# Linear attention and a two-layer network on one core: two of seven products one pair ahead, attention's product for two heads at once, new half steps

## The chip, the core and the metric

The kernel runs on one core of a Trainium2 chip. The metric is device time in microseconds (us). Five engines run beside each other, each through its own instructions in their written order: TensorE (PE in the profile; PEld is its weight load), VectorE (DVE), ScalarE (ACT), GpSimd (POOL) and SyncE (SP), which issues nearly all transfers (DMA).

## The reference

```python
q_s = exp(q - max(q, -1)); q_s = q_s / (sum(q_s, -1) + 1e-09)      # softmax over 64 features
k_s = exp(k - max(k, 2));  k_s = k_s / (sum(k_s, 2) + 1e-09)       # softmax over 576 tokens
kv  = einsum('bhsd,bhse->bhde', k_s, v)
x   = einsum('bhsd,bhde->bhse', q_s, kv)    # 8 batches, 8 heads, 576 x 64, as (4608, 512)
out = relu(x @ w_in) ** 2 @ w_out           # w_in 512 x 2048, w_out 2048 x 512
```

All data are float32.

## The kernel before, in words

A number is held as a high and a low part (both `float32r`), and a product is three matmuls: high by high, high by low, low by high. Tokens go in blocks of 512: block b is the first 512 tokens of batch b for b = 0 to 7, and block 8 holds the 64 that are left of each batch. The 16 chunks `fc` of 128 hidden features go through `x @ w_in`, relu, square and `@ w_out`.

Stages. The first phase (a list written by hand) loads and splits the weights and does attention for batches 0 and 1 and all of block 0. Block 1 takes one chunk a step: twelve matmuls of 512 columns for `h` (`h_part`), relu (ACT, L518), square (DVE, L519), split into `g_hi` (ACT, L524) and `g_lo` (DVE, L529), and two steps later twelve matmuls into the four output accumulators (`o_part`). Blocks 2 to 8 take two chunks, a *pair*, in one iteration, eight iterations a block. There `x @ w_in` goes by a scheme with seven products instead of eight, over sums and differences of weights (`s2`, `s34`, and a part of `wi` that is overwritten, built by `sum_units` on POOL, DVE and ACT during block 1) and of tokens (`combo_units`). Each product, B11, T1, B21, T2, T3, B22 and T4, is six matmuls of 256 columns (`times`, L866). They gather in three banks of PSUM: `A` (bank0), `Bk` (bank1), `E` (bank2). An iteration of before runs B11 into `A`, T1 into `E`; then ACT copies `A` into `Bk` (L917, the *seed*) and `E` into `e5` (L918); then B21 goes on in `A` and T2 in `Bk`, `u2` is copied from `Bk` (L924), T3 goes on in `Bk` and B22 in `E`; DVE adds `Bk`+`e5` and `E`+`u2` into the upper halves (L931, L932); relu and Square on ACT (L934, L938) finish chunk a. T4 goes on in `Bk`, and `relu_square` (L518, L519) finishes chunk b. Between these stand eight `triple`s, each three matmuls of 512 columns (L541 to L543), of the pair before.

Attention for batches 2 to 7 runs one block ahead, in *units* (`k_max`, `q_exp`, `parts`, ...) put at *slots* (half steps): four slots an iteration, `in_slot(slot)` to `in_slot(slot + 3)`. Two heads are a pair of 128 partitions, and two such pairs a *couple*, whose `kv` product stands at slots 2 and 16 of a block (`COUPLES`); all other slots are counted from there (`UNIT_AT`, `NINTH_AT`). The maximum of `k` over tokens needs twelve small DVE instructions per pair (`k_bound`, `k_spread`). `q` goes through a 32 x 32 transpose, out to memory and back (`q_turn`, `q_out`, `q_back`). `q_split` then splits each head's 64 partitions and puts high and low parts on opposite halves of the 128, `parts` stacks the factors likewise, and one matmul per head gives the main product in the lower and the correction in the upper 64 partitions. `joined` copies the correction (ACT, L465) and adds it (DVE, L467).

Weights of the second layer are kept in memory as split parts and streamed back through a ring of three buffers, thirteen of sixteen chunks a block (`STREAMED`, `load_out`); `s34` comes back through two buffers, one iteration after the last use of its buffer (`load_s34`).

Of the kernel before, what the change touches and what calls it, by code (L numbers as in the profile page):

```python
# [42 lines left out]
S34_AT = "o1", "o3"  # L43
SUMS_AT = 5, 9, 12, 15, 19, 22, 25, 29
# [65 lines left out]
def attention_ffn_kernel(ctx: ExitStack, tc: tile.TileContext, q, k, v, w_in, w_out, out):  # L110
# [88 lines left out]
    nc.gpsimd.memset(kvs[HALF:, 0, D:].bitcast(F32), 0.0)  # L199
    nc.gpsimd.memset(kvs[:HALF, 1, D:].bitcast(F32), 0.0)  # L200
# [43 lines left out]
    stage = {}  # L244
# [63 lines left out]
    def sum_units(p):  # L308
# [24 lines left out]
        def high_parts():  # L333
# [3 lines left out]
            s34[p] = place(S34_AT[p % 2], [P, 2, 512], "s34")  # L337
# [27 lines left out]
    def attention(b, pr):  # L365
# [7 lines left out]
        def k_max():  # L373
            st["m"] = attn_pool.tile([P, 2, D], F32, name="m")
            nc.vector.tensor_reduce(st["m"], kk.rearrange("p h j d -> p h d j"), axis=AX.X, op=ALU.max)

# [605 lines left out]
```

## Time and profile before

| | |
|---|---|
| median of 3 runs | 999.57 us (998.36 to 1000.91) |
| the profiled execution | 997.45 us |
| its span, first to last instruction | 995.4 us |
| PE busy | 878.0 us (88%), 5367 matmuls |
| DVE, ACT, POOL busy | 625.7 (63%), 507.2 (51%), 276.7 us (28%) |
| granted TensorE clock, mean | 0.964 of 2.4 GHz |
| moved by DMA | 164.06 MB, mean 165 GB/s |

Busy time of an engine is the time in which at least one of its instructions ran. Matmuls are pipelined, so the distance between two starts is shorter than the time of one, and a PE that is busy throughout can still be working below its best rate. The waits name what ended an engine's idle time.

### The profile page before, as it was taken

The page shows a single profiled execution, that of the slowest core. Times are in us where ns is not written, and L with a number is a line of the kernel's source. Part 1 is how long each engine was busy: PE and PEld are TensorE (multiplying, and loading weights), DVE is VectorE, ACT ScalarE, POOL GpSimd, SP SyncE. Part 2 cuts the span into 40 slices and gives each one's busy share as a digit, 9 for nine tenths or more (in the row PEclk, how much of TensorE's full clock was granted, in tenths as well). Part 3 has the DMA queues.
Part 4 walks back from the last instruction along what each step waited for, and adds up shares of the span by engine and source line. Part 5 has one row for each costly group of instructions (what it writes and reads, how often), then busy time and mean ns, then how long its engine had stood idle before and what let it go on. Part 6 is the DMA issues. An engine that isn't in the chain of part 4 may idle for free.

```text
span 995.4 us, 15293 instructions
## 1 busy us (share of the span) xinstructions
PE 878.0 (88%) x5367; PEld 748.0 (75%) x5367; DVE 625.7 (63%) x1273; ACT 507.2 (51%) x1038; POOL 276.7 (28%) x233
## 2 busy tenths in 40 slices
PE   8999998687768989888878989788878999999997
PEld 7777886475667877777667877777767888998996
DVE  8888879779756576657766576557776433333222
ACT  5988535354435554445544654545444544434333
POOL 5777615465411221111221221111221220111000
PEclk9999999798879999899979999999989999999999
DMA  9999345455545555555555555554544446445431
GB/s 257 282 308 238 106 143 164 141 181 176 160 132 181 156 178 158 172 158 152 163 143 192 160 179 141 174 173 149 169 136 158 131 128 186 153 132 165 148 123 47
DMA packets 124555, 164.06 MB, mean 165 GB/s; under 512 B 51776, under 2 KB 92736, under 8 KB 124480
## 3 DMA queue, kind: packets, MB, share of 16 engines
q1 hardware_dynamic: 123808, 162.41, 54.7%
q8 instruction: 42, 0.69, 0.3%
q10 hardware_dynamic: 672, 0.69, 0.2%
q14 instruction: 33, 0.27, 0.1%
HBM read 132.38 MB, written 30.67 MB: 164 GB/s over the span
## 4 chain that ended last, share of the span: by engine, by line
PE 54%; DVE 20%; ACT 13%; issue 5%; DMA 3%; POOL 2%; SPq 2%; ACTq 0%; POOLq 0%; DVEq 0%
PE bank L866 20%; PE o_ps L541 9%; PE o_ps L542 9%; PE o_ps L543 9%; ACT g_hi L524 3%; DVE r L519 2%; DVE staged L467 2%; DVE g_lo L529 2%; DVE qn L413 2%; ACT corr L465 2%; DMA qT<-bounce 1%; ACT qs L455 1%; PE bank L513 1%; PE bank L514 1%; PE bank L512 1%
## 5 line engine op out<-in xcount | busy, mean ns | idle before, releaser
L543 PE MATMUL o_ps<-wo,g_lo 128*128 128x512 f32 x576 | 231.8, 402 | 11.5 <-DVE g_lo L529 11.5
L541 PE MATMUL o_ps<-wo,g_hi 128*128 128x512 f32 x576 | 235.1, 408 | 4.9 <-ACT g_hi L524 4.9
L542 PE MATMUL o_ps<-wo,g_hi 128*128 128x512 f32 x576 | 233.1, 405 | 0.0
L529 DVE TENSOR_TENSOR g_lo<-r,g_hi 128x512 fp32r<-128x512 f32 x128 | 99.7, 779 | 103.3 <-ACT g_hi L524 102.6
L866 PE MATMUL bank<-B,wi 128*128 128x256 f32 x672 | 104.3, 292 | 51.2 <-ACT bank L917 51.2
L866 PEld LDWEIGHTS bank<-B,wi 128*128 128x128 f32 x672 | 93.3, 193 | 68.6 <-ACT bank L917 63.1
L543 PEld LDWEIGHTS o_ps<-wo,g_lo 128*128 128x128 f32 x576 | 112.5, 195 | 42.5 <-DVE g_lo L529 16.9
L541 PEld LDWEIGHTS o_ps<-wo,g_hi 128*128 128x128 f32 x576 | 114.2, 198 | 22.2 <-ACT g_hi L524 6.0
L456 POOL TENSOR_TENSOR qs<-qT,qs 64x640 fp32r<-64x640 f32 x48 | 77.5, 1615 | 189.9 <-ACT qs L455 168.9
L542 PEld LDWEIGHTS o_ps<-wo,g_hi 128*128 128x128 f32 x576 | 113.1, 196 | 15.0
L866 PE MATMUL bank<-T,wi 128*128 128x256 f32 x672 | 101.1, 286 | 17.3 <-DVE bank L931 17.3
L934 ACT ACTIVATE r<-bank 128x512 f32<-128x512 f32 x56 | 33.6, 599 | 162.0 <-DVE bank L932 162.0
L866 PE MATMUL bank<-T,s 128*128 128x256 f32 x672 | 104.3, 294 | 12.2 <-DMA s<-s_kept 8.6
L866 PEld LDWEIGHTS bank<-T,wi 128*128 128x128 f32 x672 | 89.6, 190 | 27.3 <-DVE bank L931 24.3
L866 PEld LDWEIGHTS bank<-T,s 128*128 128x128 f32 x672 | 95.2, 200 | 17.2 <-issue 8.9
L524 ACT CAST g_hi<-r 128x512 fp32r<-128x512 f32 x128 | 79.5, 621 | 46.3 <-DVE r L519 39.4
L467 DVE TENSOR_TENSOR staged<-bank,corr 64x320 f32<-64x320 f32 (+1 forms) x96 | 43.0, 448 | 88.4 <-ACT corr L465 88.1
L931 DVE TENSOR_TENSOR bank<-bank,uu 128x256 f32<-128x256 f32 x56 | 23.8, 424 | 103.4 <-PE bank L866 103.2
L263 POOL TENSOR_TENSOR B<-staged,B 128x512 fp32r<-128x512 f32 x21 | 27.8, 1323 | 204.6 <-ACT B L259 126.8
L465 ACT COPY corr<-bank 64x320 f32<-64x320 f32 (+1 forms) x96 | 38.1, 396 | 71.8 <-PE bank L461 48.0
L924 ACT COPY uu<-bank 128x256 f32<-128x256 f32 x56 | 20.8, 371 | 64.0 <-PE bank L866 64.0
L519 DVE TENSOR_TENSOR r<-r,bank 128x512 f32<-128x512 f32 x72 | 48.9, 680 | 6.1 <-ACT r L518 6.0
(186 smaller groups left out, 1464.1 us busy)
## 6 DMA issues: line engine op xcount, KB each, us to landing
wo<-out_kept SPq DMA_DIRECT2D x91, 512.0 KB, 3.6
s<-s_kept SPq DMA_DIRECT2D x56, 512.0 KB, 4.2
bounce<-tb SPq DMA_DIRECT2D x28, 320.0 KB, 2.4
qT<-bounce SPq DMA_DIRECT2D x104, 80.0 KB, 3.8
raw_i<-in_moe_w_in_dram SPq DMA_DIRECT2D x16, 512.0 KB, 6.7
raw_o<-in_moe_w_out_dram SPq DMA_DIRECT2D x16, 512.0 KB, 8.4
out_dram<-o SPq DMA_DIRECT2D x64, 128.0 KB, 2.5
out_kept<-wo SPq DMA_DIRECT2D x13, 512.0 KB, 3.7
```

The lines of the kernel that those rows point to most:

```text
L263: nc.gpsimd.tensor_tensor(t[:, 1], src, t[:, 0].bitcast(F32), op=ALU.subtract)
L456: nc.gpsimd.tensor_tensor(qs[other], src, qs[own].bitcast(F32), op=ALU.subtract)
L465: nc.scalar.copy(corr[half[h]], ps[HALF:])
L467: nc.vector.tensor_tensor(dst, ps[:HALF], corr[half[h]], op=ALU.add)
L519: nc.vector.tensor_tensor(r, r, ps, op=ALU.mult)
L524: nc.scalar.copy(g_hi, r)
L529: nc.vector.tensor_tensor(g_lo, r, g_hi.bitcast(F32), op=ALU.subtract)
L541: nc.tensor.matmul(acc, g_hi[:, ts], wo[fc][:, 0], start=(n == 0), stop=False)
L542: nc.tensor.matmul(acc, g_hi[:, ts], wo[fc][:, 1], start=False, stop=False)
L543: return nc.tensor.matmul(acc, g_lo[:, ts], wo[fc][:, 0], start=False, stop=(n == NFC - 1))
L866: nc.tensor.matmul(dst, lhs, rhs, start=start and c == n == 0, stop=c == 1 and n == 2, skip_group_check=True)
L934: nc.scalar.activation(ra, A, AF.Relu)
```

## The change

1. B11 and T1 of the next pair run inside this iteration (`ahead`): B11 after the fifth triple, T1 behind T4. `seed` follows chunk b's relu on ACT. An iteration starts with T2, B21, B22; T3 stands between the second and third triple. Chunk b's square goes from DVE to ACT (Square), in blocks 2 to 8 always and in block 1 for every second chunk. `e5` and `u2` have fixed buffers (`spare`).
2. Attention's product takes two heads at once: `kvs` holds two block-diagonal 128 x 128 factors (high and low), `q_high` and `q_low` split all 128 partitions in one instruction each, three matmuls gather in PSUM (L453), and one ACT copy per product (L454) takes the place of `joined`.
3. `k_bound` and `k_spread` run once per couple, over 256 columns, and DVE's four small copies are reductions now (`k_stats`).
4. All units and loads have new slots (`FORMER`, `LATTER` and three tables for the first couples). The sums of weights of pairs 5 to 7 move from block 1 to block 2.
5. `s34` has three buffers and is loaded an iteration earlier; chunk 6 of the second layer is streamed too (fourteen of sixteen).

The core of the diff (line numbers of the change in the text are those of the changed kernel):

```diff
-COUPLE_AT = {1: (6, 18)}
-COUPLES = 2, 16
-STREAMED = tuple(fc for fc in range(16) if fc not in (6, 14, 15))
+COUPLES = {1: (6, 17)}, (2, 15)
+STREAMED = tuple(fc for fc in range(16) if fc not in (14, 15))
-S34_AT = "o1", "o3"
-SUMS_AT = 5, 9, 12, 15, 19, 22, 25, 29
+S34_AT = "o1", "o3", "o6"
+S34_BUILT = 0, 1, 0, 1, 2, 2, 0, 1
+SUMS_AT = tuple((s, s + 2, s + 3, s + 4) for s in (5, 9, 13, 17, 21, 39, 43, 47))
...
-    parts=(0, 5), low0=(3, 8), low1=(4, 9), high=(5, 11), k_less=(-7, -1), k_exp=(-6, -1), q_split=(1, 5), k_max=(-13, -8),
...
+    k_max=(-17, -14), q_max=(-16, -9), q_less=(-16, -8), q_exp=(-15, -7), q_sum=(-13, -5), q_norm=(-10, -4),
...
     def load_s34(i):
-        if i < NFC // 2 * (B - 1):
+        if i not in (5, 6, 7) and i < NFC // 2 * (B - 1):
             p = i % (NFC // 2)
-            t = s34[p] = place(S34_AT[i % 2], [P, 2, 512], "s34")
+            t = s34[p] = place(S34_AT[i % 3], [P, 2, 512], "s34")
...
-        def product(h, ps, g0, nj):
-            qs = st["q"][h][:, :nj, g0 : g0 + 2].rearrange("p j g a -> p j (g a)")
-            nc.tensor.matmul(ps.rearrange("p (j i) -> p j i", j=nj), kvs[:, h], qs, start=True, stop=True)
-
-        def joined(h, ps, corr, at):
-            n = ps.shape[1]
-            nc.scalar.copy(corr[half[h]], ps[HALF:])
-            dst = staged(b, pr // 2)[half[h], at : at + n]
-            nc.vector.tensor_tensor(dst, ps[:HALF], corr[half[h]], op=ALU.add)
+        def product(g0, nj, at):
+            n = nj * HALF
+            ps = bank(n)
+            for i, (k, x) in enumerate(((0, 0), (0, 1), (1, 0))):
+                rhs = st["q"][x][:, :nj, g0 : g0 + 2].rearrange("p j g a -> p j (g a)")
+                dst = ps.rearrange("p (j i) -> p j i", j=nj)
+                nc.tensor.matmul(dst, kvs[:, k], rhs, start=(i == 0), stop=(i == 2))
+            nc.scalar.copy(staged(b, pr // 2)[:, at : at + n], ps)
...
-    def relu_square(ps):
+    def relu_square(ps, by_act):
         r = work.tile([P, NT], F32, name="r")
         nc.scalar.activation(r, ps, AF.Relu)
-        nc.vector.tensor_tensor(r, r, ps, op=ALU.mult)
+        if by_act:
+            nc.scalar.activation(r, r, AF.Square)
+        else:
+            nc.vector.tensor_tensor(r, r, ps, op=ALU.mult)
         return r
...
+                following = (blk, p + 1) if p + 1 < NFC // 2 else (blk + 1, 0)
+                times(Bk[:, low0], lambda i: s2[p][:, i], blk, "T2", False)
+                times(A[:, low0], lambda i: wi[fa][:, i, QUAD:], blk, "B21", False)
+                times(E[:, low0], lambda i: s34[p][:, i, QUAD:], blk, "B22", False)
+                nc.scalar.copy(u2, Bk[:, low0])
                 triple(0)
                 in_slot(slot)
+                tt(A[:, low1], E[:, low0], u2, op=ALU.add)
+                triple(1)
                 times(Bk[:, low0], lambda i: s34[p][:, i, :QUAD], blk, "T3", False)
                 tt(Bk[:, low1], Bk[:, low0], e5, op=ALU.add)
                 ra = work.tile([P, NT], F32, name="r")
                 nc.scalar.activation(ra, A, AF.Relu)
+                triple(2)
+                in_slot(slot + 1)
+                triple(3)
                 triple(4)
+                ahead(*following, 1)
                 nc.scalar.activation(ra, ra, AF.Square)
                 ga = low_part(*high_part(ra))
+                in_slot(slot + 2)
                 times(Bk[:, low0], lambda i: wi[fb][:, i, QUAD:], blk, "T4", False)
-                rb = relu_square(Bk)
+                ahead(*following, 5)
+                rb = work.tile([P, NT], F32, name="r")
+                nc.scalar.activation(rb, Bk, AF.Relu)
+                seed(following[0])
+                triple(5)
+                in_slot(slot + 3)
+                nc.scalar.activation(rb, rb, AF.Square)
                 triple(6)
                 triple(7)
+                load_s34((blk - 2) * (NFC // 2) + p + 3)
```

What moves on PE, at the passage from one iteration to the next in a middle block. Before, B11 and T1 (into bank0 and bank2) open the iteration, one triple follows, then B21 and T2:

```order
L541 MATMUL o_ps3_5020<-wo3_5052,g_hi_5153 128x512
L542 MATMUL o_ps3_5020<-wo3_5052,g_hi_5153 128x512
L543 MATMUL o_ps3_5020<-wo3_5052,g_lo_5170 128x512
L461 MATMUL bank3_90<-qs1_5146,kvs_96 128x320
L866 MATMUL bank0_87<-B11_4164,wi6_705 128x256 x6
L866 MATMUL bank2_89<-T1_4250,wi7_807 128x256 x6
L541 MATMUL o_ps0_5017<-wo4_5129,g_hi_5238 128x512
L542 MATMUL o_ps0_5017<-wo4_5129,g_hi_5238 128x512
L543 MATMUL o_ps0_5017<-wo4_5129,g_lo_5240 128x512
L866 MATMUL bank0_87<-B21_4654,wi6_705 128x256 x6
L866 MATMUL bank1_88<-T2_4718,s2_1963 128x256 x6
```
With the change, B11 of the next pair stands behind the fifth triple and T1 behind T4; `q_hi` and `q_lo` in the last rows are attention's product in three passes:

```order
L552 MATMUL o_ps0_4745<-wo3_4790,g_hi_4849 128x512
L553 MATMUL o_ps0_4745<-wo3_4790,g_hi_4849 128x512
L554 MATMUL o_ps0_4745<-wo3_4790,g_lo_4851 128x512
L877 MATMUL bank0_87<-B11_3974,wi6_705 128x256 x6
L877 MATMUL bank1_88<-T4_4564,wi5_628 128x256 x6
L877 MATMUL bank2_89<-T1_4080,wi7_807 128x256 x6
L552 MATMUL o_ps1_4746<-wo3_4790,g_hi_4849 128x512
L553 MATMUL o_ps1_4746<-wo3_4790,g_hi_4849 128x512
L554 MATMUL o_ps1_4746<-wo3_4790,g_lo_4851 128x512
L453 MATMUL bank3_90<-q_hi_4899,kvs_96 128x320
L453 MATMUL bank3_90<-q_lo_4900,kvs_96 128x320
L453 MATMUL bank3_90<-q_hi_4899,kvs_96 128x320
```
Between T1 and the next matmul that needs a seed (T2 now, B21 before) stood one triple; now three triples and, here, attention's product stand there.

On ACT, before, from the relu of chunk b (bank1) to the seeds, at the start of iteration 2 of a block (`corr` is the correction of attention's product, `kvs` its factors, `qs0` and `qs1` the split `q`):

```order
L518 ACTIVATE r_5120<-bank1_88 128x512
L465 COPY corr_5054<-bank3_90 64x256 x2
L240 CAST kvs_96<-kf_4943 64x64
L447 CAST kvs_96<-kf_4943 64x64
L240 CAST kvs_96<-kf_4943 64x64
L447 CAST kvs_96<-kf_4943 64x64
L455 CAST qs0_5143<-qT_97 64x640
L455 CAST qs1_5146<-qT_97 64x640
L524 CAST g_hi_5153<-r_5120 128x512
L917 COPY bank1_88<-bank0_87 128x256
L918 COPY uu_5155<-bank2_89 128x256
```
And with the change, from the relu of chunk a (bank0) to the copy of `u2`:

```order
L958 ACTIVATE r_4769<-bank0_87 128x512
L454 COPY staged0_4777<-bank3_90 128x320
L407 ACTIVATE qn_4756<-qn_4756 128x640
L964 ACTIVATE r_4769<-r_4769 128x512
L535 CAST g_hi_4802<-r_4769 128x512
L454 COPY staged0_4777<-bank3_90 128x256
L970 ACTIVATE r_4830<-bank1_88 128x512
L933 COPY bank1_88<-bank0_87 128x256
L934 COPY spare0_1528<-bank2_89 128x256
L974 ACTIVATE r_4830<-r_4830 128x512
L535 CAST g_hi_4849<-r_4830 128x512
L950 COPY spare0_1528<-bank1_88 128x256
```
The two seeds (bank1 from bank0, `spare0` from bank2) stood behind eight instructions of attention and the split of chunk b; they now come straight behind chunk b's relu, and the split of chunk b comes after them.

On DVE, before, the seven instructions of attention and of the token sums between `g_lo` of one iteration and the two additions (L931, L932) of the next:

```order
L529 TENSOR_TENSOR g_lo_4708<-r_4668,g_hi_4691 128x512
L426 TENSOR_TENSOR qn_4526<-qn_4526,qs_4624 128x640
L281 TENSOR_TENSOR staged0_3927<-staged1_4424,staged0_3927 128x512
L283 TENSOR_TENSOR staged0_3927<-staged0_3927 128x256 x2
L430 STREAM_TRANSPOSE tb_4745<-qn_4526 128x5x4x32
L413 TENSOR_TENSOR qn_4749<-qt1_84,qm_4689 128x2x5x64
L287 TENSOR_TENSOR staged1_4424<-staged1_4424,staged0_3927 128x512
L931 TENSOR_TENSOR bank1_88<-bank1_88,uu_4693 128x256
L932 TENSOR_TENSOR bank0_87<-bank2_89,uu_4693 128x256
```
With the change, from one pair of additions (L953, L956) to the next:

```order
L953 TENSOR_TENSOR bank0_87<-bank2_89,spare0_1528 128x256
L956 TENSOR_TENSOR bank1_88<-bank1_88,spare0_1528 128x256
L421 STREAM_TRANSPOSE tb_4389<-qn_4174 128x5x4x32
L399 TENSOR_REDUCE qm_4393<-qt1_84 128x10
L540 TENSOR_TENSOR g_lo_4415<-r_4383,g_hi_4413 128x512
L392 TENSOR_TENSOR kt1_80<-kt1_80,spare1_1529 128x640
L404 TENSOR_TENSOR qn_4424<-qt1_84,qm_4393 128x2x5x64
L287 TENSOR_TENSOR staged0_3735<-staged1_4167,staged0_3735 128x512
L289 TENSOR_TENSOR staged0_3735<-staged0_3735 128x256 x2
L540 TENSOR_TENSOR g_lo_4464<-r_4438,g_hi_4462 128x512
L953 TENSOR_TENSOR bank0_87<-bank2_89,spare0_1528 128x256
L956 TENSOR_TENSOR bank1_88<-bank1_88,spare0_1528 128x256
```
The additions now stand right behind `g_lo` here, and the units that stood ahead of them lie after the additions of the iteration before.

## Rows read from the trace of the kernel before

**Rows 1.** Windows: first phase, block 1, blocks 2, 4, 6 and 8.
```profile
core 0: us, PE busy (x) PEld busy (x) DVE busy (x) ACT busy (x) POOL busy (x), PEclk, DMA share, GB/s
0.00:126.46 126.46, 123.16 (x712) 98.84 (x712) 105.74 (x196) 97.19 (x182) 87.53 (x86) 1.00 0.84 234
126.46:238.66 112.20, 95.54 (x457) 76.81 (x456) 92.23 (x177) 50.35 (x104) 56.22 (x47) 0.92 0.48 157
238.66:367.78 129.12, 99.11 (x625) 84.79 (x624) 86.35 (x175) 59.50 (x127) 30.89 (x25) 0.92 0.57 167
480.54:593.68 113.14, 96.53 (x625) 82.76 (x624) 74.60 (x164) 57.35 (x122) 22.71 (x18) 0.95 0.55 164
706.37:814.55 108.18, 95.81 (x625) 82.64 (x624) 63.21 (x141) 56.66 (x122) 23.33 (x18) 0.97 0.47 143
899.01:983.40 84.39, 84.39 (x530) 76.23 (x529) 24.63 (x44) 33.18 (x68) 1.29 (x1) 1.00 0.39 120
```

**Rows 2.** Windows, same columns: iteration 0 of block 2, iteration 2 of block 4.
```profile
238.66:261.07 22.41, 15.03 (x108) 12.70 (x106) 20.42 (x41) 8.91 (x21) 10.84 (x10) 0.77 0.63 202
508.94:526.72 17.78, 12.90 (x71) 11.37 (x70) 10.69 (x21) 8.31 (x19) 3.08 (x2) 0.81 0.53 163
```

**Rows 3.** Timeline of PE: where two iterations of block 7 start (start us, us).
```profile
867.36 0.88 PE L866 MATMUL bank<-B,wi 128*128 128x256 f32 x6
877.90 0.88 PE L866 MATMUL bank<-B,wi 128*128 128x256 f32 x6
```

**Rows 4.** Timeline of PE: attention's products in block 4, and what follows them.
```profile
490.47 0.80 PE L500 MATMUL bank<-vt,ke 128*64 128x65 f32 x20
...
491.78 0.98 PE L866 MATMUL bank<-T,wi 128*128 128x256 f32 x6
...
506.42 0.31 PE L461 MATMUL bank<-qs,kvs 128*128 128x320 f32 x1
506.57 0.92 PE L866 MATMUL bank<-T,wi 128*128 128x256 f32 x6
```

**Rows 5.** Waits of PE in blocks 3 to 5 (total us, times, longest).
```profile
PE bank L866 <- ACT bank L917: 29.1, 18, 4.9
PE bank L866 <- DVE bank L931: 11.5, 9, 1.9
PE o_ps L541 <- ACT g_hi L524: 2.9, 3, 1.0
```

**Rows 6.** Timeline of ACT around the longest wait in block 4.
```profile
514.31 0.72 ACT L455 CAST qs<-qT 64x640 fp32r<-64x640 f32 x1 [0.76 <-DMA qT<-bounce]
...
515.70 0.36 ACT L917 COPY bank<-bank 128x256 f32<-128x256 f32 x1
```

**Rows 7.** Waits of PE in block 1.
```profile
PE o_ps L543 <- DVE g_lo L529: 10.2, 3, 4.4
```

**Rows 8.** Waits of PE in block 2.
```profile
PE bank L866 <- DMA s<-s_kept: 8.6, 1, 8.6
```

**Rows 9.** Groups by line, blocks 3 to 5: busy us, mean ns, idle before.
```profile
L529 DVE TENSOR_TENSOR g_lo<-r,g_hi 128x512 fp32r<-128x512 f32 x48 | 35.5, 739 | 35.1 <-ACT g_hi L524 34.9
L467 DVE TENSOR_TENSOR staged<-bank,corr 64x320 f32<-64x320 f32 (+1 forms) x48 | 21.5, 448 | 50.8 <-ACT corr L465 50.7
L465 ACT COPY corr<-bank 64x320 f32<-64x320 f32 (+1 forms) x48 | 19.0, 397 | 38.5 <-PE bank L461 29.4 <-DVE staged L467 8.7
L519 DVE TENSOR_TENSOR r<-r,bank 128x512 f32<-128x512 f32 x24 | 16.3, 679 | 0.0
L938 ACT ACTIVATE r<-r 128x512 f32<-128x512 f32 x25 | 15.8, 631 | 0.3
```

**Rows 10.** Groups by line on DVE in block 1.
```profile
L529 DVE TENSOR_TENSOR g_lo<-r,g_hi 128x512 fp32r<-128x512 f32 x14 | 14.1, 1005 | 1.3 <-ACT g_hi L524 1.3
L384 DVE COPY m<-m 32x4 f32<-32x4 f32 x16 | 7.4, 465 | 0.3
L321 DVE TENSOR_TENSOR sums<-w_sum 128x256 f32<-128x256 f32 x7 | 5.5, 791 | 6.4 <-POOL w_sum L315 6.4
```

More of the change, by code (lines that the diff above doesn't have):

```diff
@@ L318, in sums @@
             wa, wb = t[a], t[b]
-            s = t["s"] = place("m3", [P, 4, QUAD], "sums", F32)
+            s = t["s"] = place("m3" if p < 5 else "l2", [P, 4, QUAD], "sums", F32)
             tt = nc.vector.tensor_tensor
@@ L444, in parts @@
             for h in range(2):
-                own, other = half[h], half[1 - h]
-                split(kvs[own, h, :D], kvs[own, h, D:], st["kf"][own])
-                nc.scalar.copy(kvs[other, h, :D], st["kf"][own])
-        def q_split():
-            st["q"] = []
-            for h in range(2):
-                own, other = half[h], half[1 - h]
-                qs = attn_pool.tile([P, LOW, 4, BLK], F32R, name=f"qs{h}", tag="q_lo" if h else "q_hi", bufs=1)
-                src = qT[own].rearrange("p g j a -> p j g a")
-                nc.scalar.copy(qs[own], src)
-                nc.gpsimd.tensor_tensor(qs[other], src, qs[own].bitcast(F32), op=ALU.subtract)
-                st["q"].append(qs)
@@ L479, in high, with q_high @@
-        def high():
-            ps = bank(2 * QUAD).rearrange("p (h i) -> p h i", h=2)
-            for h in range(2):
-                product(h, ps[:, h], 2, HIGH)
-            for h in range(2):
-                joined(h, ps[:, h], st["corr"][:, LOW * HALF :], H1[pr % 2])
+                own = half[h]
+                split(kvs[own, 0, own], kvs[own, 1, own], st["kf"][own])
+        def q_high():
+            st["q"] = [attn_pool.tile([P, LOW, 4, BLK], F32R, name=x, tag=x, bufs=1) for x in ("q_hi", "q_lo")]
+            nc.scalar.copy(st["q"][0], qT.rearrange("p g j a -> p j g a"))
@@ L808, in attention_ffn_kernel @@
     tc.no_sync_barrier()
+    spare.extend(w_pool.tile([P, 512], F32, name=f"spare{i}", tag="w", bufs=WB) for i in range(3))
     steps = [(blk, fc) for blk in range(B + 1) for fc in range(NFC)]
@@ L906, in triple, with ahead, seed @@
                 load_out()
-        waiting = [1, NFC // 2 - 1, [gs.pop(2 * NFC - 2), None]]
+        e5, u2 = spare[0][:, low0], spare[0][:, low1]
+        def ahead(blk, p, own):
+            if blk > B:
+                return
+            fa, fb = 2 * p, 2 * p + 1
+            if own == 1:
+                times(A[:, low0], lambda i: wi[fa][:, i, :QUAD], blk, "B11", True)
+            else:
+                times(E[:, low0], lambda i: wi[fb][:, i, :QUAD], blk, "T1", True)
+        def seed(blk):
+            if blk <= B:
+                nc.scalar.copy(Bk[:, low0], A[:, low0])
+                nc.scalar.copy(e5, E[:, low0])
+        waiting = [1, NFC // 2 - 1, [gs.pop(2 * NFC - 2), None]]
+        for own in 1, 5:
+            ahead(2, 0, own)
+        seed(2)
+        waiting[2][1] = low_part(*mid)
+        late_loads = []
         for blk in range(2, B + 1):
@@ L924, in attention_ffn_kernel @@
-                nc.scalar.copy(u2, Bk[:, low0])
-                for i in 1, 2, 3:
-                    triple(i)
-                in_slot(slot + 1)
+                tt(A[:, low1], E[:, low0], u2, op=ALU.add)
+                triple(1)
                 times(Bk[:, low0], lambda i: s34[p][:, i, :QUAD], blk, "T3", False)
-                times(E[:, low0], lambda i: s34[p][:, i, QUAD:], blk, "B22", False)
-                load_s34((blk - 2) * (NFC // 2) + p + 2)
                 tt(Bk[:, low1], Bk[:, low0], e5, op=ALU.add)
-                tt(A[:, low1], E[:, low0], u2, op=ALU.add)
```

193 lines of the change are left out of this document (100 added, 93 removed).

## The prediction, made before the changed kernel ran

> **What bounds the kernel now.** I read the windows by stage first, then the timeline of PE where it is dense, then PE's waits, and last the groups by line of the engines that PE waits for. Windows: blocks 7 and 8, which hold no attention, keep PE busy throughout at a granted clock of 1.00, 84.39 us for block 8; blocks 3 to 5 take (706.37 - 367.78) / 3 = 112.9 us each, and in block 4 PE, DVE and ACT are busy for 96.5, 74.6 and 57.4 us of 113.1, so none is full [rows 1]. The timeline gives the price of an iteration without stalls: 877.90 - 867.36 = 10.54 us [rows 3]. It has 42 matmuls of 256 columns and 24 of 512, 23040 columns, so 0.457 ns a column. Attention's own matmuls cost PE little: the `kv` product of a couple holds it from 490.47 to 491.78, 1.31 us, and a product of 320 columns 0.15 us [rows 4], as the price by columns says. A block with attention would thus need 8 x 10.54 + 2 x 1.31 + 4 x (2 x 0.15 + 2 x 0.12) = 89.1 us of PE. The other 23.8 us are waits and what follows them: in blocks 3 to 5 PE waits 29.1 us for the seed (L917), 11.5 us for the addition on DVE (L931), 2.9 us for `g_hi` [rows 5], and its clock falls, as in iteration 2 of block 4, 17.78 us at 0.81 [rows 2]. So the chain through in-order ACT and DVE sets these blocks, not the amount of work. Blocks 1 and 2 are different. DVE is busy for 92.23 us of block 1's 112.20 [rows 1] and for 20.42 of the 22.41 us of block 2's iteration 0 [rows 2]: 112.65 of 134.61 us, 84%, and PE waits there for `g_lo` on DVE, 10.2 us in block 1 [rows 7].
>
> **Blocks 3 to 5: the seed.** The wait of 4.9 us in iteration 2 shows the mechanism. The seed copies `A`, which was ready early, but stands behind attention's instructions on ACT: `qs` waits 0.76 us for a transfer, then runs to 515.0, `g_hi` follows, and the copy starts at 515.70 [rows 6]. The orders show the seeds now straight behind chunk b's relu. From T4's end PE has T1 (6 x 0.117 = 0.70 us) and three triples (9 x 0.234 = 2.1) to do before T2, 2.8 us; relu, at most Square's 0.63 [rows 9], and the copy, 0.36 [rows 6], take 1.0. The seed's 9.7 us a block go. The addition behind T3 now stands ahead of that half step's units on DVE, and PE has three triples and B11 between T3 and T4 (2.8 us, against B22 and two triples, 2.1): its 3.8 us a block should mostly go too. What is late next: `u2`, which ACT copies after chunk b's `g_hi`, and `g_hi` must wait for triple 7 of the pair before (two buffers), so ACT reaches `u2` about when T2 ends; T3 comes 2.8 us after that, which covers it.
>
> **The work that is added and removed**, per block. PE: three passes in place of two, 4 x (0.15 + 0.12) = 1.1 us more, on the path: 90.2 us. DVE: eight squares of 0.679 and sixteen additions of `joined` at 0.448 go [rows 9], 5.4 + 7.2; the maxima, once per couple, I leave as reserve. 74.6 becomes at most 62 of 92. ACT: eight Squares of 0.631 come, eight of sixteen copies of 0.397 go [rows 9]. `q_high` on 128 partitions lies between one `qs` of 0.72 [rows 6] and two; I take one, since ACT's time goes by columns: 0.397 on 64 partitions for 320 at most, 0.631 on 128 for 512 [rows 9]. 57.4 + 5.0 - 3.2 - 2.9 = 56.3. Both hide behind PE; uncovered they would cost what they exceed 90 by, nothing. `joined` also went ACT, DVE, ACT, DVE: DVE idles 50.7 us in three blocks for `corr` and ACT 8.7 for `staged` [rows 9]. That ends, since the new product is one copy on ACT. Loads: `s34` is asked for an iteration earlier, behind the stream of `wo` on SP, and one chunk a block more is streamed; the transfers' share, 0.55 [rows 1], becomes about 0.55 x 112.9 / 92 = 0.68 plus a thirtieth, 0.70. The first phase ran at 0.84, so I cost this at nothing; if a load came late its price would be like the one wait for `s34`, 8.6 us [rows 8].
>
> What stays of stalls in blocks 3 to 5 lies between nothing and the waits on DVE and `g_hi` unchanged, (11.5 + 2.9) / 3 = 4.8 us. I take 2.2: **92.4 us** each, 90.2 to 95. Block 6 has fewer units (DVE 63.2 us [rows 1]): 91.5.
>
> **Block 1 and block 2's iteration 0.** PE's price by columns: 360 matmuls of 512, 84.3; two `kv`, 2.6; four pairs, 3.2; an iteration and its `kv`, 11.9: 102 us. DVE loses eight squares and iteration 0's, 6.1, and sixteen additions of `joined`, 7.2 [rows 9]. Three pairs' sums of weights move out: an addition of 0.791 [rows 10] and three of that size or less, 2.4 to 9.5, I take 6. The maxima are spread three times instead of five; the copies alone cost 7.4 us [rows 10], of which 3 to all go, I take 5. So 112.65 - 24.3 = 88.4 us, and at the old share of 84% a stretch of **106 us**, against 134.6; between PE's 102 and, with the sure savings alone (18.7), 112.
>
> **The rest of block 2** took 129.12 - 22.41 = 106.7 us. PE's price is 90.2 - 11.9 = 78.3. `s34` now comes three iterations ahead, so its 8.6 us [rows 8] should go; three pairs' sums come in, beside PE. I take 83, between 78.3 and 87.
>
> **The sum.** First phase 126.46, unchanged; 106; 83; 3 x 92.4 = 277.2; 91.5; blocks 7 and 8, 983.40 - 814.55 = 168.85, which wait for nothing already; the tail, 995.40 - 983.40 = 12.0. Together 865.0, with the 2.05 us around the span 867.1, against the profiled 997.45. The median of the runs lies 0.21% above that execution, so the forecast is **869 us**. The bounds give 852 to 890.
>
> **A rule weighed.** `g_lo` takes 739 ns in blocks 3 to 5 [rows 9] but 1005 in block 1 [rows 10], where POOL is busy for half of the time [rows 1]. The Trainium skill, "SBUF — State Buffer", section "Who interferes with whom", says that VectorE and GpSimd share one pair of ports, that an instruction holds it to its end, and that a VectorE instruction with two SBUF inputs contends with GpSimd's reads. The trace agrees with it as far as 266 ns go. By that rule the sums that move into block 2 bring DVE waits there, and the time would be nearer to 887 than to 869; the first rival prices this from rows.
>
> **The rivals.**
> *DVE shut out in block 2.* Block 1 has POOL busy for 56 us [rows 1]; three of its eight pairs' sums are at most 21. Iterations 2 to 4 of block 2 then hold DVE work near PE's 11.3 us, and if POOL's 21 us come on top of it, nearly all reaches PE: 18 us, **887**. For it: the 1005 ns. Against: those sums were a large part of what made DVE wait in block 1.
> *Only the seed's wait goes.* The units are as many engine instructions in order as before, and another wait takes the place of the additions. Blocks 3 to 5 give 112.9 - 9.7 + 1.1 = 104.3, block 6 99.6, the stretch of block 1 128, the rest of block 2 98: 126.5 + 128 + 98 + 312.9 + 99.6 + 168.9 + 12 = 946, **950** as a median.
> *The seed comes late everywhere, slower.* T2 now opens every iteration and needs a copy that ACT can make only after T4, relu and all that ACT has ahead. If ACT reaches it late, all 56 iterations lose, those of blocks 7 and 8 too. It decides from (997.45 - 867.1) / 56 = 2.3 us of PE's wait each, that is ACT 1.8 + 2.3 = 4.1 us behind; at 2.5 us the time is 867 + 140, **1009**. Against: in block 8 ACT is busy for 33 of 84 us [rows 1].
> *No change* (within 0.3%, about what a measurement of this kernel can tell) would need all waits to reappear elsewhere. That the orders do not hold what the change says is excluded by the rows shown.
>
> **How the numbers follow.** Forecast 0.70, DVE shut out 0.14, only the seed 0.10, slower 0.04, no change 0.02. The first two fill 850 to 902: the lower end is the bound by PE's prices, the upper one 21 us on the upper half of the forecast's own range (881). The remaining 0.16, and what little of the first two lies outside, stays out. Faster: 0.70 + 0.14 + 0.10 = 0.94.
>
> **What would show it.** Blocks 3 to 5 near 92 us with PE's clock at 1.00; no wait for the seed (L933) over 1 us; PE's waits in these blocks below 7 us in all, against 43.5 in the three rows [rows 5]. DVE below 63 us a block, ACT near 56. Block 1 with iteration 0 near 106 us and DVE's share still above 80%. It is wrong if iterations of blocks 3 to 5 stay over 12.5 us, if blocks 7 and 8 lose their 10.54, or if PE waits for transfers more than once.

## The result and the profile after

The changed kernel took **861.48 us** (median of 4 runs, 860.15 to 863.11) against 1000.1 us (4 runs) for the kernel before on the same chip: ratio 0.8617, 95% interval 0.8597 to 0.8637. The profiled execution took 862.06 us with a span of 860.3. The forecast was 869 us, 850 to 902.

Windows by stage of the changed kernel: the stretch and its length, busy time of PE, PEld, DVE, ACT and POOL with instructions, PE's granted clock, DMA share, GB/s. The cuts are the first phase's old end (126.46), the start of T2 in each block's first iteration, and the tail.

```profile
0.00:126.46 126.46, 119.20 (x685) 93.96 (x686) 102.57 (x192) 94.80 (x177) 83.81 (x84) 1.00 0.85 234
126.46:224.70 98.24, 97.13 (x503) 79.38 (x503) 85.70 (x150) 50.51 (x98) 45.77 (x38) 1.00 0.63 200
224.70:318.02 93.32, 91.50 (x634) 81.52 (x633) 69.44 (x130) 56.28 (x119) 34.14 (x29) 1.00 0.71 209
318.02:408.72 90.70, 90.70 (x633) 81.77 (x632) 56.70 (x116) 53.05 (x109) 16.12 (x14) 1.00 0.72 209
408.72:499.42 90.70, 90.70 (x633) 81.77 (x632) 56.62 (x116) 53.06 (x109) 16.04 (x14) 1.00 0.73 209
499.42:590.12 90.70, 90.70 (x633) 81.76 (x632) 57.16 (x116) 53.17 (x109) 16.57 (x14) 1.00 0.73 209
590.12:680.82 90.70, 90.70 (x633) 81.77 (x632) 41.17 (x86) 50.90 (x105) 15.78 (x14) 1.00 0.57 173
680.82:765.35 84.53, 84.53 (x529) 76.15 (x528) 21.93 (x40) 41.30 (x81) 8.97 (x8) 1.00 0.51 162
765.35:849.89 84.54, 84.54 (x524) 75.86 (x523) 19.99 (x35) 37.97 (x73) 0.56 (x1) 1.00 0.38 125
849.89:860.30 10.41, 4.33 (x19) 3.17 (x17) 0.69 (x1) 1.76 (x3) 0.00 (x0) 0.85 0.39 102
```

Beside [rows 1] the reader sees that blocks 3 to 6 all take 90.70 us and PE is busy for 90.70 of them, at a clock of 1.00: TensorE is the bound there. DVE fell from 74.60 to 56.6 us a block, ACT from 57.35 to 53.1. PE's waits of blocks 1 and 2 (in us, times, longest) are all that is left behind the first phase; for blocks 3 to 5 the same view, which showed 43.5 us in its three largest rows before [rows 5], shows none:

```profile
PE bank L877 <- ACT r L958: 1.3, 1, 1.3
PE bank L453 <- POOL q_lo L445: 1.1, 1, 1.1
PE bank L877 <- ACT bank L933: 0.4, 1, 0.4
```

ACT's timeline in iteration 2 of block 5 (start, us, line, what, idle before) stands against [rows 6]: the seed (L933, L934) comes straight behind chunk b's relu (L970), and Square, `g_hi` and attention's casts come after it.

```profile
519.51 0.37 ACT L454 COPY staged<-bank 128x256 f32<-128x256 f32 x1 [0.16 <-PE bank L453]
520.22 0.60 ACT L970 ACTIVATE r<-bank 128x512 f32<-128x512 f32 x1 [0.34 <-PE bank L877]
520.85 0.36 ACT L933 COPY bank<-bank 128x256 f32<-128x256 f32 x1
521.12 0.38 ACT L934 COPY spare<-bank 128x256 f32<-128x256 f32 x1
521.39 0.65 ACT L974 ACTIVATE r<-r 128x512 f32<-128x512 f32 x1
```

### The profile page after: what moved, and what is told of

It reads as the page before. It is cut to its first block, busy times and chain, and to the rows that moved or that the text cites. A ratio compares the mean times of both kernels' runs of the same rounds, so it can differ in the third digit from the quotient of the medians.

```text
span 860.3 us, 14979 instructions
## 1 busy us (share of the span) xinstructions
PE 844.0 (98%) x5415; PEld 737.1 (86%) x5415; DVE 512.0 (60%) x981; ACT 492.8 (57%) x982; POOL 237.8 (28%) x209
## 4 chain that ended last, share of the span: by engine, by line
PE 80%; DMA 10%; DVE 5%; SPq 2%; issue 1%; ACT 1%; POOL 1%; ACTq 0%; DVEq 0%
PE bank L877 32%; PE o_ps L554 13%; PE o_ps L552 13%; PE o_ps L553 13%; DMA qt<-in_q_dram 4%; PE bank L453 2%; PE bank L508 2%; PE bank L522 1%; PE bank L520 1%; PE bank L521 1%; DMA kt<-in_k_dram 1%; DMA v_whole<-in_v_dram 1%; DVE g_lo L540 1%; DMA raw_o<-in_moe_w_out_dram 1%; DMA raw_i<-in_moe_w_in_dram 1%
## 5 line engine op out<-in xcount | busy, mean ns | idle before, releaser
L552 PE MATMUL o_ps<-wo,g_hi 128*128 128x512 f32 x576 | 228.0, 396 | 0.0
L553 PE MATMUL o_ps<-wo,g_hi 128*128 128x512 f32 x576 | 227.0, 394 | 0.4 <-POOL wo L765 0.4
L552 PEld LDWEIGHTS o_ps<-wo,g_hi 128*128 128x128 f32 x576 | 109.4, 190 | 16.4
L553 PEld LDWEIGHTS o_ps<-wo,g_hi 128*128 128x128 f32 x576 | 108.4, 188 | 16.9 <-POOL wo L765 0.8
L877 PE MATMUL bank<-T,s 128*128 128x256 f32 x672 | 98.0, 281 | 0.5 <-ACT bank L933 0.4
L877 PE MATMUL bank<-T,wi 128*128 128x256 f32 x672 | 90.0, 283 | 0.0
L445 POOL TENSOR_TENSOR q_lo<-qT,q_hi 128x640 fp32r<-128x640 f32 x24 | 39.2, 1633 | 174.7 <-ACT q_hi L441 173.8
L958 ACT ACTIVATE r<-bank 128x512 f32<-128x512 f32 x56 | 33.6, 600 | 89.1 <-DVE bank L953 89.1
L956 DVE TENSOR_TENSOR bank<-bank,spare 128x256 f32<-128x256 f32 x56 | 24.2, 432 | 68.8 <-PE bank L877 68.5
L269 POOL TENSOR_TENSOR B<-staged,B 128x512 fp32r<-128x512 f32 x21 | 29.1, 1388 | 124.6 <-ACT B L265 121.2
L970 ACT ACTIVATE r<-bank 128x512 f32<-128x512 f32 x56 | 33.4, 597 | 42.8 <-PE bank L877 42.7
L877 PE MATMUL bank<-B,s 128*128 128x256 f32 x336 | 49.4, 283 | 0.0
L520 PE MATMUL bank<-x,wi 128*128 128x512 f32 x120 | 47.7, 397 | 0.0
L269 POOL TENSOR_TENSOR T<-staged,T 128x512 fp32r<-128x512 f32 x21 | 27.3, 1300 | 73.0 <-ACT T L265 67.4
```

What stands on the lines that cost most here:

```text
L269: nc.gpsimd.tensor_tensor(t[:, 1], src, t[:, 0].bitcast(F32), op=ALU.subtract)
L445: nc.gpsimd.tensor_tensor(lo, qT.rearrange("p g j a -> p j g a"), hi.bitcast(F32), op=ALU.subtract)
L520: nc.tensor.matmul(ps, wi[fc][:, 0, sl], xh, start=(cc == 0), stop=False)
L552: nc.tensor.matmul(acc, g_hi[:, ts], wo[fc][:, 0], start=(n == 0), stop=False)
L553: nc.tensor.matmul(acc, g_hi[:, ts], wo[fc][:, 1], start=False, stop=False)
L877: nc.tensor.matmul(dst, lhs, rhs, start=start and c == n == 0, stop=c == 1 and n == 2, skip_group_check=True)
```

## The experiments

The theory at the outset was the prediction's: B11 and T1 a pair ahead, with the seed early on ACT, are the main cause. Its rival: the lighter queues (product, half steps) are. Twelve more kernels were run. To see where each gains or loses, the trace of its profiled execution was cut at the start of the first `kv` product (L500 before, L508 after) of blocks 1, 3 and 6: **A** is from block 1's to block 3's (before: 377.7 - 140.1 = 237.6 us), **B** from there to block 6's, three whole blocks (716.3 - 377.7 = 338.6). Each ratio goes by runs of the kernel before that were taken beside it, with medians from 996.26 to 1000.1 us.

| kernel | median us | ratio to before, 95% interval | up to A | A | B | rest of span |
|---|---|---|---|---|---|---|
| before | 1000.1 | 1 | 140.1 | 237.6 | 338.6 | 279.1 |
| changed | 861.48 | 0.8617 (0.8597 to 0.8637) | 146.4 | 178.7 | 272.1 | 263.1 |
| e1 old order | 869.8 | 0.8716 (0.8691 to 0.8742) | 146.2 | 185.5 | 274.1 | 262.7 |
| e2 seed late | 918.36 | 0.9204 (0.9176 to 0.9232) | 145.8 | 184.8 | 298.8 | 287.4 |
| e3 old product | 891.59 | 0.8939 (0.8898 to 0.8981) | 143.6 | 202.3 | 279.9 | 263.2 |
| e4 square on DVE | 869.14 | 0.8712 (0.8686 to 0.8737) | 146.2 | 184.4 | 273.7 | 262.8 |
| e5 = e1 + e4 | 866.5 | 0.8697 (0.8670 to 0.8724) | 145.2 | 184.8 | 272.3 | 263.0 |
| e6 before + square | 998.83 | 1.0029 (1.0008 to 1.0050) | 141.8 | 237.9 | 338.1 | 278.9 |
| e7 before + order | 978.54 | 0.9820 (0.9794 to 0.9846) | 141.8 | 236.7 | 327.5 | 272.9 |
| e8 sums in block 1 | 887.64 | 0.8910 (0.8887 to 0.8933) | 144.2 | 204.9 | 272.1 | 263.0 |
| e9 before + product | 942.9 | 0.9448 (0.9406 to 0.9490) | 140.3 | 213.7 | 314.8 | 272.2 |
| e10 = e3 + e5 | 926.32 | 0.9270 (0.9223 to 0.9317) | 143.7 | 210.8 | 297.2 | 270.6 |
| e11 k maxima per pair | 866.84 | 0.8690 (0.8656 to 0.8725) | 146.5 | 181.4 | 273.6 | 262.9 |
| e12 before, one unit moved | 984.18 | 0.9857 (0.9814 to 0.9900) | 142.5 | 235.5 | 328.7 | 275.3 |

**The order taken back (e1).** The iteration of the kernel before in the changed kernel:

```diff
+                ahead(blk, p, 1)
+                ahead(blk, p, 5)
+                seed(blk)
+                waiting[2][1] = low_part(*mid)
                 triple(0)
                 in_slot(slot)
...
-                ahead(*following, 1)
...
-                ahead(*following, 5)
...
-                seed(following[0])
...
```

> The changed kernel with the iteration order of the kernel before: an iteration begins with its own B11 and T1, and the two seed copies come behind g_hi of the chunk before. Slots, the three-pass product, the k maxima and the square on ScalarE stay as changed. Theory (the order of the products is the main cause): T2's successors wait for the seed again, 1 to 2 us in each of the 56 iterations, so blocks 3 to 5 go from 90.7 to 100 to 104 us, blocks 7 and 8 from 84.5 to 92 to 98, and the run takes 920 to 955 us. Rival (relief of VectorE and ScalarE by the new slots and the three-pass product is the main cause): the seed's wait shrinks by itself, blocks 3 to 5 stay at 94 us or less and the run takes 890 us or less.

869.8 us, ratio 0.8716: the rival held and the theory fell. B loses 2.0 us, A 6.8; blocks 7 and 8 lose nothing.

**The seed late (e2).**

```diff
-                seed(following[0])
                 triple(5)
...
                 waiting = [blk, p, [ga, low_part(*high_part(rb))]]
+                seed(following[0])
```

> The changed kernel with only the two seed copies moved: they are issued at the end of the iteration, behind g_hi of chunk b, and not ahead of chunk b's square; B11 and T1 stay a pair ahead. Theory (the place of the seed on ScalarE counts as much as the products' place): the copies end 0.7 to 1.5 us behind T2's turn, every iteration grows by that much, blocks 7 and 8 go from 84.5 to 90 to 96 us and the run takes 900 to 945 us. Rival (once B11 and T1 are made ahead the seed has slack wherever it stands): no wait for the seed over 0.5 us, 861 to 870 us.

918.36 us, in the theory's range. PE's waits and the windows of blocks 7 and 8:

```profile
721.39:814.47 93.08, 86.69 (x528) 75.52 (x529) 21.91 (x41) 41.24 (x82) 8.96 (x7) 1.00 0.46 147
814.47:907.55 93.08, 87.49 (x527) 76.19 (x528) 19.69 (x35) 37.85 (x74) 0.00 (x0) 1.00 0.36 114
PE bank L877 <- ACT bank L933: 12.8, 16, 0.8
```

All 16 iterations wait 0.8 us, and a block takes 93.08 us in place of 84.5, so 1.07 an iteration. With B11 and T1 ahead, T2 opens the iteration and the seed has no work of PE to hide behind but what stands between T4 and T2. The new order thus gives the seed less room unless the copies also move up; the two belong together.

**The square on VectorE (e4), and with the old order (e5).**

```diff
-                rb = work.tile([P, NT], F32, name="r")
-                nc.scalar.activation(rb, Bk, AF.Relu)
+                rb = relu_square(Bk, False)
...
-                nc.scalar.activation(rb, rb, AF.Square)
```

> The changed kernel with chunk b's square back on VectorE, where it reads bank Bk, so that the seed copy into Bk comes behind it. Theory (the square on ScalarE is what lets the seed be issued early): the seed waits for VectorE's queue, 0.5 to 1.5 us in iterations of blocks 2 to 6 and less in 7 and 8, where VectorE is nearly idle: blocks 3 to 5 at 93 to 99 us, blocks 7 and 8 under 86.5, 870 to 905 us in all. Rival (the square's engine does not matter with the products ahead): 860 to 864 us.

> The changed kernel with both the old iteration order (as in e1) and chunk b's square on VectorE (as in e4); the slots, the three-pass product, the k maxima and the loads stay as changed. Theory A (order and square are two cures for one late seed, so that either alone is enough and e1 and e4 lost only 8 us each): without both the seed waits 1 us or more per iteration in blocks 2 to 6 again, 905 to 945 us. Theory B (the product and the new slots are what took the wait away, and order and square add a few us each): the losses of e1 and e4 add, 875 to 885 us.

e4 took 869.14 us, just below its theory's range; nearly all of the loss is in A (184.4 against 178.7), where VectorE is full. e5 took 866.5, less than either theory gave, and cannot be told from e1 or e4. Its B of 272.3 us is the changed kernel's 272.1, and PE waits for nothing in it:

```profile
330.00:602.30 272.30, 272.30 (x1897) 244.04 (x1896) 194.89 (x372) 143.65 (x304) 50.91 (x39) 1.00 0.72 209
```

So with the other parts in place, order and square are worth nothing in blocks 3 to 5 and about 6 us in A.

**Order and square alone on the kernel before (e6, e7).** e6 has e4's edit the other way round; e7 the changed iteration, with `ahead`, `seed` and the square on ACT, and the last sums of tokens at other half steps:

```diff
+        c1 -= blk == 1
...
-            (c1 + 12, ("t3", "T2h", "T2l")), (c1 + 13, ("t4", "T3h", "T3l")), (c1 + 14, ("B22h", "B22l")),
-            (c1 + 15, ("T4h", "T4l")),
+            (c1 + 12, ("t3", "T2h", "T2l")), (c1 + 13, ("B22h", "B22l")), (c1 + 14, ("T3h", "T3l")),
+            (c1 + 15, ("t4", "T4h", "T4l")),
...
```

> The kernel before with one edit: chunk b's square is made on ScalarE from the relu's result, no longer on VectorE from the bank. Order, slots and product are those of before. Theory A: the seed's wait of 29.1 us in blocks 3 to 5 mostly goes, 930 to 960 us. Theory B: ScalarE and VectorE are too full in blocks 2 to 5 with the joins, the wait only moves, 975 to 1000 us.

> The kernel before with the changed kernel's iteration: B11 and T1 a pair ahead, the seed between chunk b's relu and its square, the square on ScalarE; slots, two-pass product, k maxima and loads as before, only the last sums of x (B22, T3, t4, T4) up to one half step earlier or later so that they exist when the new order needs them. Theory A: most of the gain comes with the iteration alone, 895 to 935 us. Theory B: the rest of the change (product, slots) is needed, 945 to 980 us. In both, blocks 7 and 8 keep 10.5 us per iteration.

The square alone gains nothing (1.0029). With the order it gives 1.8%, just inside theory B. PE's waits in e7's B:

```profile
PE bank L867 <- ACT uu L941: 19.1, 9, 5.3
PE bank L867 <- ACT bank L924: 12.7, 6, 3.7
PE bank L867 <- ACT r L950: 3.0, 7, 0.5
```

The seed's 29.1 us [rows 5] become 12.7, but `u2` (L941) now waits 19.1: the same casts on ACT (`qs`, which wait 12.1 us for q's transfer in this stretch) stand ahead of the next thing in line.

**The product (e3, e9).** e3 puts the old two-head product back into the changed kernel, e9 puts the new one into the kernel before; of e9's edit, its half steps:

```diff
-    parts=(0, 5), low0=(3, 8), low1=(4, 9), high=(5, 11), ... q_split=(1, 5), ...
+    parts=(0, 5), low=(4, 9), high=(5, 11), ... q_high=(1, 5), q_low=(1, 5), ...
...
```

> The changed kernel with the product for two heads as it was before: two joined copies of the split parts, low and high in two bank passes instead of three products into one bank. TensorE has 512 columns less per pair of heads, by the rows 0.9 to 1.1 us per block side. Theory (TensorE is the only bound of blocks 2 to 6, and ScalarE and VectorE have room for the joins): 5 to 8 us faster than the changed kernel, 853 to 857 us. Rival (the joins bring ScalarE's and VectorE's queues back to the point where TensorE waits for their copies): waits for L453 to L529's successors of 1 us or more in several iterations, 862 to 885 us.

> The kernel before with the product for two heads in three passes: one cast and one subtraction of q for both heads, two copies of kv's parts in place of four, one copy out of the bank in place of a copy and an addition per head; at the old half steps (low where the second of the two low products stood). Order, square, sums, k maxima and loads as before. Theory C (the joins, in which ScalarE, VectorE and TensorE wait for each other in turn, make the seed late): most of what is left open goes here, 905 to 950 us. Theory D (the half steps are the cause: several units and a DMA's wait stand in one half step ahead of g_hi and the seed): 970 to 995 us.

e3 lost 30 us, more than the rival gave: 23.6 in A, 7.8 in B. Half steps for the joins were chosen for this test alone, so a better table may lose less. What ends PE's waits from 120 to 340 us, first of all the join's addition (L458):

```profile
PE bank L452 <- DVE staged L458: 7.4, 4, 3.0
PE bank L521 <- ACT kt L395: 4.2, 1, 4.2
PE bank L890 <- ACT bank L946: 3.9, 4, 1.7
```

e9 took 942.9 us, ratio 0.9448: theory C's range, and the largest gain of what was put alone into the kernel before in e6, e7, e9 and e12 (23.9 us in A, 23.8 in B). Most of what PE still waits in its B stands in one row, and ACT's timeline shows why (the seed is L904):

```profile
PE bank L853 <- ACT bank L904: 23.8, 9, 7.3
```

```profile
474.34 0.51 ACT L240 CAST kvs<-kf 64x64 fp32r<-64x64 f32 x2
481.92 0.72 ACT L450 CAST q_hi<-qT 128x640 fp32r<-128x640 f32 x1 [7.07 <-DMA qT<-bounce]
482.55 0.61 ACT L511 CAST g_hi<-r 128x512 fp32r<-128x512 f32 x1
```

ACT stands for 7 us before `q_hi`, since q is not back from memory; `g_hi` and the seed, whose data are there, queue behind it.

**The half steps (e10, e12).** e10 keeps of the change only the half steps, the sums' move, the k maxima and the loads. e12 moves one unit of the kernel before, the second pair's `q_split`, by two half steps:

```diff
-    parts=(0, 5), ... q_split=(1, 5), ...
+    parts=(0, 5), ... q_split=(1, 7), ...
```

> The changed kernel with the old iteration order, the square on VectorE and the old two-pass product (e3 and e5 together): what stays of the change are the half steps, the moved sums with their third place, the k maxima per two pairs and the loads. Theory C: the joins bring the late seed back, 930 to 975 us. Theory D: the losses of e3 and e5 add to each other, 890 to 915 us.

> The kernel before with one number changed: the second pair's q_split (two casts on ScalarE and two subtractions on GpSimd) two half steps later, at 7 in place of 5, where it no longer stands behind the four copies of kv's parts and q's transfer has had more time. Theory D: the seed is late mainly because of this half step, the 29.1 us in blocks 3 to 5 fall under 15, 950 to 980 us. Theory C: the wait only moves to the joins, 990 to 1002 us.

e10: 0.9270, between the two ranges: neither C nor D alone. With the old order and the square on VectorE in all four, the parts nearly add: A is 237.6 before, 213.7 with the product (-23.9), 210.8 with e10's parts (-26.8), 184.8 with both (-52.8); B is 338.6, 314.8 (-23.8), 297.2 (-41.4) and 272.3 (-66.3). PE's waits in e10's B are 17.5 us in all, against 48.8 before (the 43.5 of [rows 5] and 5.3 in two smaller rows):

```profile
PE bank L890 <- ACT bank L946: 8.9, 9, 1.4
PE bank L890 <- DVE bank L968: 5.4, 3, 2.0
PE o_ps L567 <- DVE g_lo L553: 3.2, 6, 0.6
```

Here order and square do count: from e10 to e3 the ratio falls by 0.033, from e5 to the changed kernel by 0.008. e12 gains 1.4% by one number and just misses D's range; in its B the seed's wait falls to 22.3 us, not under 15, and its longest to 2.6 us in place of 4.9:

```profile
PE bank L866 <- ACT bank L917: 22.3, 18, 2.6
PE bank L866 <- DVE bank L931: 11.5, 9, 1.9
```

**The sums in block 1 (e8).** All eight pairs' sums in block 1 at the old half steps, built in two places, with the old loads (`s34` of iteration 1 is asked for behind iteration 0):

```diff
-S34_BUILT = 0, 1, 0, 1, 2, 2, 0, 1
-SUMS_AT = tuple((s, s + 2, s + 3, s + 4) for s in (5, 9, 13, 17, 21, 39, 43, 47))
+S34_BUILT = 0, 1, 0, 1, 0, 1, 0, 1
+SUMS_AT = tuple((s, s + 1, s + 2, s + 3) for s in (5, 9, 12, 15, 19, 22, 25, 29))
...
```

> The changed kernel with all eight pairs' weight sums made in block 1 again, at the old half steps, in the two old places, and their loads behind block 1. Theory (block 1 was bound by VectorE's queue, which the move of three pairs' sums relieves; block 2 pays for them): block 1 with iteration 0 grows by 4 to 10 us, the rest of block 2 falls by 1 to 3 us, 864 to 870 us. Rival (the move bought nothing, since TensorE was the bound of block 1 once the k maxima and q's copies were lighter): 858 to 862 us.

887.64 us: block 1 is longer, as the theory had it, but the edit cost 26 us where 3 to 9 were expected, all of it in A (204.9 against 178.7). Windows of block 1 and block 2's iterations 0 and 1; DVE's `g_lo` in block 1; the waits of PE up to 275 us:

```profile
126.50:238.08 111.58, 96.60 (x494) 77.58 (x492) 99.66 (x163) 52.95 (x105) 61.51 (x51) 0.98 0.59 194
238.08:252.78 14.70, 14.70 (x107) 13.26 (x107) 5.15 (x13) 6.73 (x15) 5.40 (x5) 0.81 0.23 77
252.78:274.66 21.88, 13.99 (x74) 12.46 (x72) 8.21 (x13) 6.04 (x13) 0.00 (x0) 0.77 0.51 131
```

```profile
L538 DVE TENSOR_TENSOR g_lo<-r,g_hi 128x512 fp32r<-128x512 f32 x16 | 18.2, 1137 | 0.0
```

```profile
PE bank L875 <- DMA s<-s_kept: 7.9, 1, 7.9
PE bank L875 <- ACT bank L931: 7.1, 1, 7.1
PE o_ps L552 <- DVE g_lo L538: 4.4, 4, 2.6
```

Block 1 is 13 us longer with DVE busy for 99.66 us (85.70 after the change), and iteration 1 of block 2 takes 21.88 us, 7.9 of it waiting for `s34`, whose load stands behind iteration 0. Another 7.1 us are the first seed of block 2, late on ACT (L931). The old half steps of the sums meet the new ones of all other units here, so a table made for both may lose less.

**The k maxima (e11).**

```diff
-        for u, name in zip(k_stats(c == 0, 2), ("k_bound", "k_spread")):
-            at(base + when[name], u)
+        for n in range(c == 0, 2):
+            for u, name in zip(k_stats(n, n + 1), ("k_bound", "k_spread")):
+                at(base + when[name], u)
```

> The changed kernel with the small steps of k's maxima made once per pair again, in the same half steps (k_bound and k_spread twice in a row). Theory: VectorE has room in blocks 2 to 6 (57 of 90.7 us busy), TensorE stays the bound, and only block 1 with 86 of 98 us busy may give 1 to 3 us: 860 to 865 us. Rival: the longer rows of small instructions stand ahead of g_lo and the additions into the banks and come out in full on TensorE, 2 to 3 us for each of 12 couples: 875 to 895 us.

866.84 us, between the two, nearer to the theory: 2.7 us in A, and 0.5 a block in B.

No version tried beats the changed kernel.

## Why the prediction was right in number and wrong in cause

Term by term, from the windows above. Block 1's `kv` product starts 6.3 us later than before, and block 1 with iteration 0 (its T2 starts at 224.70, the next one's at 236.78) takes 98.24 + 12.08 from the old end of the first phase:

| term | forecast | measured |
|---|---|---|
| first phase | 126.46 | 126.46 + 6.3 |
| block 1 and iteration 0 | 106 | 110.3 - 6.3 = 104.0 |
| rest of block 2 | 83 | 81.2 |
| blocks 3 to 5, each | 92.4 | 90.70 |
| block 6 | 91.5 | 90.70 |
| blocks 7 and 8 | 168.85 | 169.07 |
| tail | 12.0 | 10.41 |

The cuts at T2 lie behind B11 and T1 of a block's first pair, 12 x 0.117 = 1.4 us by the prediction's price: most of the tail's gain is this shift, and the row of block 1 and iteration 0 holds it as a cost.

- **Blocks 3 to 5: the size was right, the step failed in its cause.** "The orders show the seeds now straight behind chunk b's relu. [...] The seed's 9.7 us a block go." They go with the old order too (e5). The order takes them away only halfway on the kernel before (e7), where the wait passes on to `u2`. I took the seed's place for the cure, and did not ask what the change does to the units ahead of it: I priced `q_high`'s length, as busy time, and not what a lighter or later unit does to the seed. The row that I showed of them, `qs` waiting for its transfer [rows 6], is the smaller part. From the end of chunk b's relu (509.85) to the seed (515.70) ACT takes 5.85 us there: 0.76 idle for the transfer, 1.08 idle for the join's addition on DVE (L467), and the other 4.0 are the length of the units. In B of the kernel before ACT waits 1.4 us for q's transfer in all; with the lighter product alone it waits 18.1 (e9); in the changed kernel it waits 5.6, and PE does not wait. ACT's rows of the relu and the join in block 4, and its waits for q in B (before, e9, changed):

```profile
509.25 0.60 ACT L518 ACTIVATE r<-bank 128x512 f32<-128x512 f32 x1
511.33 0.37 ACT L465 COPY corr<-bank 64x256 f32<-64x256 f32 x1 [1.08 <-DVE staged L467]
ACT qs L455 <- DMA qT<-bounce: 1.4, 2, 0.8
ACT q_hi L450 <- DMA qT<-bounce: 18.1, 3, 7.1
ACT q_hi L441 <- DMA qT<-bounce: 5.6, 3, 2.1
```

The price of PE's own work, 90.2 us by columns against 90.70, gave the right time whichever part removed the waits. That the time came out as the story of the seed had it was luck.

- **The product** had in blocks 3 to 5 a price (1.1 us a block of PE) and no gain; its end of the ping-pong between ACT and DVE was named, and left without a term. Only block 1's sum gave it one, 7.2 us of DVE. Alone it is worth 5.5% of the kernel before (e9), and its removal costs 30 us (e3).
- **The units' new half steps** had no step at all, and the earlier transfers I put at nothing. e10's parts (half steps, loads, k maxima and the sums' move) are worth 7.3% without the rest. What of the 41.4 us in B falls to the half steps and what to the loads was not separated, so this part of the cause stays open; one unit two half steps later is worth 9.9 on the kernel before (e12, 338.6 - 328.7), the k maxima 1.5 in the changed one (e11).
- **Block 1.** The sums' move was taken at 6 us of DVE, and `s34`'s wait at 8.6. The wait was right (7.9 in e8); the rest of e8's 26.2 us in A is some 18, three times the 6. It holds the late seed's 7.1 us and the lower clock behind both waits too, so it is no price of the sums alone.
- **The rivals.** DVE was not shut out in block 2: with POOL busy for 34 of 93 us PE waits 1.7 us there. "Only the seed's wait goes" is what e7 shows with the old product and half steps: another wait, `u2`'s, comes in. In the changed kernel its premise fails, since there are fewer instructions (DVE 116 a block in place of 164, ACT 109 in place of 122 in block 4). The slower rival is real, at 1.07 us an iteration in place of 2.3 or more, and hangs on the two copies' place (e2).
- **A rule weighed.** `g_lo` takes 783 ns in blocks 3 to 5 of the changed kernel, where POOL is busy for 16 of 90.7 us, 1071 in its block 1 (45.8 of 98.2), and 1137 in e8 (61.5 of 111.6). The Trainium skill, "SBUF — State Buffer", section "Who interferes with whom", has VectorE and GpSimd share a pair of ports; the three rows agree, though no run varied GpSimd's work alone. Its price in blocks 3 to 5 was covered by PE.

The stated signs came: PE's clock at 1.00, no wait for the seed over 0.4 us, DVE under 63 us in each of blocks 3 to 5, ACT at 53 (56 was stated), DVE busy for 91.13 of the 110.32 us of block 1 and iteration 0 (83%), iterations of blocks 3 to 5 at 12.45 us or less (the bound was 12.5), blocks 7 and 8 at 10.57 (10.54 before), no wait of PE for a transfer in blocks 2 to 8. None of them could tell the causes apart, and none watched the first phase, the one term that came out clearly worse.

## What to carry to other kernels

Where an in-order engine makes something urgent late, look first at what stands ahead of it, how long it is and what it waits for; making such units lighter was worth more here than moving the urgent one (5.5% in e9 against 1.8% in e7), and moving one of them by two half steps nearly as much (1.4% in e12). A sum that goes down to the busiest engine's own work will hit the time whenever all waits go, and so says nothing on which part removed them: only runs with one part undone, and with one part alone, do. Parts that remove the same wait are not worth what each seems to be (order and square: 3.3% of the kernel before with the old product, 0.8% with the new one).

## What the runs showed that was not expected

In several of these traces waits cost more than their length, since the granted clock falls after them. In B of the kernel before PE waits 48.8 us and is busy for 289.67, at 0.96, a mean of the two levels 2.4 and 1.2 GHz:

```profile
377.70:716.30 338.60, 289.67 (x1875) 248.40 (x1874) 224.72 (x492) 171.99 (x364) 68.41 (x51) 0.96 0.55 164
```

The changed kernel does that work and 3.3 us of products more (1.1 a block) in 272.1 us, so PE lost 289.67 - 268.8 = 21 us while busy, beside the 48.8. A clock of 0.96 explains some 12 of them (4% of 289.67); the rest is not named. The 7.9 us wait of e8 shows it in one iteration (13.99 us busy for what takes 11.34 in the changed kernel, at 0.77). In e12 PE's first wait in B is 1.98 us, and the stretch from 386.50 to 390.00 us behind it is at 0.51, the lower level:

```profile
385.77 1.05 PE L866 MATMUL bank<-B,wi 128*128 128x256 f32 x6 [1.98 <-ACT bank L917]
386.50:390.00 3.50, 3.50 (x14) 3.06 (x13) 1.79 (x2) 0.37 (x1) 1.15 (x1) 0.51 0.65 165
```

In e2, 0.8 us in every iteration left the clock at 1.00, and so did the one wait of 1.3 us in block 2 of the changed kernel.

The first phase reaches block 1's `kv` product at 143.6 to 146.5 us in the nine kernels with the new half steps (the changed one and e1 to e5, e8, e10 and e11) and at 140.1 to 142.5 in the five with the old ones. In the changed kernel's profile ACT waits 5.0 us there for the weights' transfers (`raw_i`), against 0.5 before. These are single executions: e12 edits nothing in the first phase, and is 2.4 us later than the kernel before all the same. So how much of the 6.3 us is the change's, and which edit's, stays open.
